# Scale columns written by ScalarE a slot before their scatter, and one-tile scatters for the last two batches

## The chip, the cores and the metric

The kernel runs on one core of one Trainium2 chip. The core has five engines: TensorE (PE, matmuls, with a weight-load part PEld), VectorE (DVE), ScalarE (ACT), GpSimd (POOL) and SyncE (SP), which issues most transfers. POOL issues the indirect transfers, those whose row numbers lie in a tile. Every engine works through its own list of instructions in order and waits on the others by semaphores. The metric is device time in microseconds (us) of one execution; less is better.

## The reference

Two stages. The first filters a sequence: `x` has 8 batches of 2496 tokens with 256 columns, and each batch is transformed along the tokens, multiplied by a filter, and transformed back. The second is a mixture of eight experts on the 19968 filtered tokens.

```python
y = np.fft.irfft(np.fft.rfft(x, axis=1) * (filt_r + 1j*filt_i), n=2496, axis=1)
x = y.reshape(8*2496, 256)
logits = x @ w_gate                        # 8 experts
e_idx = np.argmax(logits, axis=1)
gate_w = softmax(logits)[n, e_idx]
eom = 1 / (1 + np.exp(-(x @ w_output_gate)))
for e in range(8):
    mask = e_idx == e
    h = np.maximum(x[mask] @ w1[e], 0)     # 256 -> 1024
    out[mask] = gate_w[mask, None] * eom[mask, e, None] * (h @ w2[e])
```

All is float32. Each token goes through one expert only, and its row of the output is multiplied by one number, its output scale.

## The kernel before

**Tokens.** A batch is cut into 22 tiles of up to 117 tokens, 11 pairs. The filter is done as a two-step transform forwards and a two-step transform back, with a trip through memory between the steps. The last step, `inv_a` (matmul at L587, ScalarE's copy at L588), puts a pair of tiles into the ring `yring` in SBUF. The ring holds 44 rows of 258 columns a partition: two batches, so batch 7 overwrites the rows of batch 5. A row has 256 columns of the token, then the token's number (written by VectorE at L639), then its output scale.

**Routing.** When a batch is in the ring, `gates` (L624) has computed its logits, and the generator `route` takes one step a slot for five slots: the chosen expert, the place of each token in its expert's list (`dest`), and in its last step the output scale, a reciprocal that VectorE writes into the ring for all 22 tiles at once (L683).

**Scatter.** `scatter(b, q)` (L690) issues, on POOL, two indirect transfers for pair q: 117 rows each go from the ring to the sorted list `srt` in memory. Each waits for `dest` and for the ring's row.

**Experts.** The class `Experts` works through the sorted list in blocks of 512 tokens (later some of 256). A block of 512 takes 8 steps. In each step `up` multiplies by w1 (L119 to L121 into `ph`), ScalarE and VectorE read the result out of PSUM (`hh` L288, `hl` L289), and `down` multiplies by w2. Two steps after the last `up` the block's output is scaled (L331, later L327 and L328) and four indirect transfers on POOL write it to `out` (L333). The tokens of block i+2 are loaded from `srt` (`xs`, L233) in the third step of block i. All of it is unrolled. The first 12 blocks may hold only tokens of batches 0 to 3; the others wait for all scatters.

**Order.** The order on each engine is written by hand: `for n in range(-5, last + LS + TP + 1)` is a loop over slots, and `plan` names, for each slot, which function works on which batch and pair. With TP = 11, LB = 15, LI = 33, LS = 52 and last = 77:

- pair q of batch b: `inv_a` in slot 33 + 11b + q, scatter in slot 52 + 11b + q (for batch 7 one slot later); so batch 5 is scattered in slots 107 to 117, batch 6 in 118 to 128, batch 7 in 130 to 140;
- the last step of `route`, with the reciprocal, in slot 105 for batch 5, 116 for batch 6 and 128 for batch 7;
- the experts' step n in slot 105 + n: block i begins in slot 105 + 8i, and its four output transfers stand in slot 114 + 8i;
- the slot loop ends after slot 140; then the experts go on by themselves, first in `while ffn.n < 8 * NEARLY` (NEARLY = 12 blocks). The tokens of block 12, the first that waits for all scatters, are loaded in step 82, which would be slot 187.

No slot has a barrier. An engine that has no wait runs ahead of the others through its own list. From slot 105 on POOL's list holds nothing but the scatters and the output transfers.

Of the kernel before, what the change touches and what calls it, by code (L numbers as in the profile page):

```python
# [10 lines left out]
F32 = mybir.dt.float32  # L11
# [9 lines left out]
P = 128  # L21
B, S, D = 8, 2496, 256
# [3 lines left out]
NT = 22  # L26
TP = NT // 2
KP = KC // 2
# [6 lines left out]
NBLK = NFULL + 21  # L35
RING = 22
GT = 4
LATE = 7
NOID = 1 << 20

# [359 lines left out]
def build(tc, x, filt_r, filt_i, wg, wo, w1, w2, c_small, c_fb, c_ids, out):  # L400
    nc = tc.nc
    V, A, G = nc.vector, nc.scalar, nc.gpsimd
    with ExitStack() as ctx, ExitStack() as right, ExitStack() as early, ExitStack() as early_c, ExitStack() as early_x, ExitStack() as outer:
        def pool(stack, name, bufs, **kw):
            return stack.enter_context(tc.tile_pool(name=name, bufs=bufs, reuse_waits="tile", **kw))
# [3 lines left out]
        rt = pool(ctx, "rt", 1)  # L409
# [95 lines left out]
        def rows(b, t0, t1):  # L505

            o = NT * (b % 2)
            return yr[:, o + t0:o + t1]

        xt, U, Yt, T, yT, ys, lg, dest = [{} for _ in range(8)]  # L510
        XCH = [(t, min(t + 4, NT)) for t in range(0, NT, 4)]

        def load_x(b, tp):
# [82 lines left out]
        def split_y(b, tp):  # L596

            g, i = divmod(tp, GT)
            if i == 0:
                return  # L600
            if i == 1:
                ys[b, g] = [w2p.tile([P, 2 * GT, D // 32, 32], F32R, tag="ys" + c, name=f"ys{c}{b}_{tp}", bufs=1) for c in "hl"]
                split_pair(b, tp - 1)
            split_pair(b, tp)

        def split_pair(b, tp):
            g, i = divmod(tp, GT)
            h, l = [a[:, 2 * i:2 * i + 2] for a in ys[b, g]]
# [4 lines left out]
        def gates(b, tp):  # L613
            g, i = divmod(tp, GT)
            if i < GT - 1 and tp < TP - 1:
                return
# [3 lines left out]
            m = 2 * i + 2  # L620
            o = psL.tile([P, 2 * GT, 32], F32, tag="l", name=f"pl{b}_{g}")[:, 0:m, :]
            for k in range(D // 32):
# [4 lines left out]
        def route(b):  # L627
            n = 117
# [33 lines left out]
            eo = tl([NT], "eo")  # L662
# [17 lines left out]

            V.tensor_scalar(out=eo[:n], in0=eo[:n], scalar1=1.0, scalar2=None, op0=ALU.add)
            V.scalar_tensor_tensor(out=eo[:n], in0=sm[:n], scalar=1e-9, in1=eo[:n], op0=ALU.add, op1=ALU.mult)
            V.reciprocal(out=rows(b, 0, NT)[:n, :, D + 1:D + 2], in_=eo[:n].unsqueeze(2))  # L683
            dest[b] = di

        def scatter(b, q):
            di = dest[b]
            for t in (2 * q, 2 * q + 1):
                k = 39 * rows_of(t)
                i = G.indirect_dma_start(out=srt[:, :], out_offset=IndirectOffsetOnAxis(ap=di[:k, t:t + 1], axis=0),  # L690
                                         in_=rows(b, t, t + 1)[:k, 0, :], in_offset=None, bounds_check=8 * CAP - 1, oob_is_err=False)
                tc.declare_no_dep(i.ins, group="scatter", reason="tokens go to rows of their own")
                tc.add_to_no_dep_group("scatter", i.ins)
                if b >= EARLY:
                    tc.declare_no_dep(i.ins, group="early", reason="early blocks hold tokens of the first batches alone")
                    tc.add_to_no_dep_group("late", i.ins)

        LB = TP + 4
        LI = LB + TP + 7
        LS = LI + TP + 8  # L700
        last = (B - 1) * TP
        routes = []
        ffn = Experts(nc, tc, srt, w1, w2, out)

        def count(name):
# [8 lines left out]
        def table_late():  # L714

            V.tensor_copy(out=pos.unsqueeze(2), in_=st["base"][0:1, :, NT:NT + 1])
            cnt = count("cnt")
            yield from block_table(nc, tabs, cnt, numbers, "f", tables, 9, limit=NFULL - NEARLY, taken=tables[1])
            took = tabs.tile([P, 8], F32, name="took")
            V.tensor_tensor(out=took, in0=tables[1], in1=tables[3], op=ALU.add)  # L720
            V.tensor_scalar(out=took, in0=took, scalar1=2.0, scalar2=None, op0=ALU.mult)
            yield from block_table(nc, tabs, cnt, numbers, "g", tables, 8, taken=took)
            ffn.blocks += [(tables[2], i) for i in range(NFULL - NEARLY)]
            ffn.blocks += [(tables[4], i) for i in range(NBLK - NFULL)]
# [11 lines left out]
        def routing(n):  # L736
# [3 lines left out]
        plan = (  # L740
            (-5, TP, load_x), (1, TP, store_a), (LI - 4, TP, load_t), (LB - 2, KP, load_u), (LB + 3, KP, store_w),
            (LS, TP, scatter), (LB + 1, KP, filt), (LI + 1, TP, trans_y), (0, TP, fwd_a),
            (LB, KP, fwd_b), (0, 0, experts), (LB + 2, KP, inv_b), (LI + 3, TP, gates),
            (LI, TP, inv_a), (LI + 2, TP, split_y), (0, 0, routing),
        )
        for n in range(-5, last + LS + TP + 1):
            if n in (-3, 6, 13, 16):
                constants((-3, 6, 13, 16).index(n))
            if n == 3:
                nc.sync.dma_start(out=small[:, 120:664], in_=c_small[:, 120:664])  # L750
            if n == 8:
                V.tensor_copy(out=tri, in_=small[:, 256:384])
            if n in (9, 13, 16, 19):
                finish_constants((9, 13, 16, 19).index(n))
            if n == n_raw:
                early_x.close()
                ffn.open_raw(pool(right, "wraw", 1, side="right"))
            if n == n_first:
                early_c.close()
                ffn.open_first(pool(right, "xio", 1, side="right"), pool(right, "w1p", 1, side="right"))  # L760
            if n == n_ffn:
                early.close()
                tabs = pool(ctx, "tabs", 1)
                padz = tabs.tile([P, 2, ROW], F32, name="padz")
                G.memset(padz, 0.0)
                G.memset(padz[:, :, D:D + 1].bitcast(I32), NOID)
                ffn.open(pool(ctx, "wsp", 1), pool(ctx, "fio", 3), pool(ctx, "fhid", 4),
                         pool(ctx, "psh", 2, space=PSUM), pool(ctx, "pso", 1, space=PSUM))
            for off, cnt, fn in plan:
                if not cnt:  # L770
                    fn(n)
                b, i = divmod(n - off, TP)
                if fn in (gates, scatter) and n - off >= LATE * TP:
                    b, i = divmod(n - off - 1, TP)
                    if b < LATE:
                        continue
                if 0 <= b < B and i < cnt:
                    fn(b, i)
                    if fn is gates and i == TP - 1:
                        routes.append(route(b))  # L780
                        if b == EARLY - 1:
                            routes.append(table_early())
                        if b == B - 1:
                            routes.append(table_late())
            if n == n_raw + 1:
                begin = ffn.start(0, NSURE)
            if n > n_raw:
                next(begin, 0)
# [3 lines left out]
        outer.close()  # L792
        ffn.widen(pool(right, "pso2", 1, space=PSUM, side="right"))
        while ffn.n < 8 * NEARLY:
            ffn.step()

        for e in range(E + 1):
# [38 lines left out]
```

## Time and profile before

| what | value |
|---|---|
| median of 3 runs | 1422.84 us (1418.94 to 1425.73) |
| the profiled execution's own time | 1424.8 us |
| its span, first to last instruction | 1423.0 us |
| PE busy | 1316.1 us, 92% of the span |
| VectorE, ScalarE, POOL busy | 964.5, 805.4 and 439.1 us |
| TensorE's granted clock, mean | 0.960 of full speed |
| scatters (L690) | 176, 190.6 us on POOL |
| output transfers (L333) | 164, 166.0 us on POOL |

The span is the profiled execution's own time less 1.8 us ahead of the first and behind the last instruction. Busy time of matmuls is modelled at its ends, so a busy PE is not a PE at its peak. In the rows below, a bracket such as `[8.05 <-remote]` says how long the engine stood idle before the instruction and what released it; "remote" and "another core or an unknown queue" mean that the profile saw the releasing semaphore event but not who sent it, and "issue" that no waiting is recorded.

### The profile page before, as it was taken

Reading aid. Unit: us, or ns where it says so; the run is one execution under the profiler, and the core shown is the slowest. Engines: PE = TensorE matmul, PEld = TensorE weight load, DVE = VectorE, ACT = ScalarE, POOL = GpSimd, SP = SyncE. Lnnn points to the kernel's source line nnn. Section 1 sums busy time; section 2 is a strip of 40 time slices with the busy share of each in tenths; the row PEclk is TensorE's granted clock in tenths of the full one; section 3 lists DMA queues with packets and bytes.
Section 4 is the critical chain, followed back from the end, with each engine's and each line's share of the span. In section 5 each row is a group of like instructions: output and inputs, shape, how many; then the busy total and the mean of one; then the engine's idle time right before and its main releaser. Section 6 shows DMA issues by size and latency. Waiting matters only on the chain.

```text
span 1423.0 us, 22968 instructions
## 1 busy us (share of the span) xinstructions
PE 1316.1 (92%) x6596; PEld 1055.5 (74%) x6596; DVE 964.5 (68%) x1739; ACT 805.4 (57%) x1530; POOL 439.1 (31%) x425
## 2 busy tenths in 40 slices
PE   5689998998888866999999999999999999999997
PEld 2356666666566554888888888888888888999997
DVE  0346887778977453666666667666666666888885
ACT  2578887786654332455554544544555554667764
POOL 2122276677863246221221212112121121211221
PEclk8799999998999787999999999999999999999999
DMA  8999999997965134333444433334232332465521
GB/s 243 260 320 339 320 330 328 335 340 249 307 181 138 42 101 114 78 90 86 116 104 121 118 82 82 84 103 119 68 82 38 75 91 80 119 161 145 156 47 32
DMA packets 335963, 221.48 MB, mean 156 GB/s; under 512 B 209482, under 2 KB 298524, under 8 KB 335768
## 3 DMA queue, kind: packets, MB, share of 16 engines
q1 hardware_dynamic: 316408, 177.66, 45.5%
q0 software_dynamic: 19424, 42.31, 8.9%
q8 instruction: 54, 0.88, 0.3%
q14 instruction: 77, 0.63, 0.1%
HBM read 193.21 MB, written 86.42 MB: 197 GB/s over the span
## 4 chain that ended last, share of the span: by engine, by line
PE 77%; DMA 10%; DVE 5%; another core or an unknown queue 3%; issue 3%; ACT 2%; SPq 0%; POOL 0%; ACTq 0%; DVEq 0%; POOLq 0%
PE po L316 19%; PE ph L120 11%; PE ph L119 11%; PE ph L121 10%; PE po L315 8%; DMA u<-da 7%; PE py L587 3%; PE pl L624 3%; PE pb L548 3%; PE pw L566 3%; PE pa L527 2%; DMA da<-s 1%; DMA x<-in_x 1%; PE po L318 1%
## 5 line engine op out<-in xcount | busy, mean ns | idle before, releaser
L288 ACT ACTIVATE hh<-ph 128x512 fp32r<-128x512 f32 x328 | 196.5, 599 | 404.4 <-PE ph L121 340.2
L316 PE MATMUL po<-w2hl,hh 128*128 128x512 f32 x1152 | 419.1, 398 | 0.0
L289 DVE SCALAR_TENSOR_TENSOR hl<-ph,hh 128x512 fp32r<-128x512 f32 x328 | 226.1, 689 | 269.7 <-ACT hh L288 219.2
L333 POOL DMA_INDIRECT out<-ob,meta x164 | 166.0, 1012 | 743.0 <-DVE ob L328 626.7
L119 PE MATMUL ph<-xph,w1h 128*128 128x512 f32 (+1 forms) x800 | 292.2, 365 | 11.9 <-issue 6.8
L120 PE MATMUL ph<-xpl,w1h 128*128 128x512 f32 (+1 forms) x800 | 285.9, 357 | 2.9 <-issue 2.2
L121 PE MATMUL ph<-xph,w1l 128*128 128x512 f32 (+1 forms) x800 | 284.9, 356 | 1.6 <-issue 1.5
L315 PE MATMUL po<-w2hl,hl 128*128 128x256 f32 x1008 | 283.4, 281 | 0.0
L316 PEld LDWEIGHTS po<-w2hl,hh 128*128 128x128 f32 x1152 | 216.1, 189 | 47.2
L690 POOL DMA_INDIRECT srt<-yring,di x176 | 190.6, 1083 | 69.4 <-issue 48.0
L315 PEld LDWEIGHTS po<-w2hl,hl 128*128 128x128 f32 x1008 | 190.4, 189 | 9.7
L119 PEld LDWEIGHTS ph<-xph,w1h 128*128 128x128 f32 x800 | 152.5, 191 | 31.4 <-issue 10.2
L120 PEld LDWEIGHTS ph<-xpl,w1h 128*128 128x128 f32 x800 | 152.1, 190 | 31.4 <-issue 7.5
L121 PEld LDWEIGHTS ph<-xph,w1l 128*128 128x128 f32 x800 | 152.4, 190 | 24.5 <-issue 2.2
L258 DVE TENSOR_TENSOR w1l<-w1raw,w1h 128x512 fp32r<-128x512 f32 x200 | 138.8, 694 | 0.0
L258 DVE TENSOR_TENSOR w2hl<-w2raw,w2hl 128x512 fp32r<-128x512 f32 x200 | 136.9, 684 | 0.4
L257 ACT CAST w1h<-w1raw 128x512 fp32r<-128x512 f32 x200 | 124.2, 621 | 0.1
L257 ACT CAST w2hl<-w2raw 128x512 fp32r<-128x512 f32 x200 | 123.0, 615 | 0.0
L554 POOL TENSOR_TENSOR vs<-vs,fi 128x512 f32<-128x512 f32 x56 | 72.2, 1290 | 161.3 <-ACT vs L551 153.4
L548 PEld LDWEIGHTS pb<-u,fb 128*128 128x128 f32 x320 | 59.3, 192 | 81.5 <-issue 34.3
L527 PE MATMUL pa<-x,small 117*120 117x512 f32 (+1 forms) x176 | 98.0, 648 | 17.7 <-ACT s L529 11.5
L548 PE MATMUL pb<-u,fb 128*128 128x256 f32 x320 | 86.3, 392 | 28.2 <-DMA u<-da 24.6
(180 smaller groups left out, 1798.5 us busy)
## 6 DMA issues: line engine op xcount, KB each, us to landing
w1raw<-in_moe_w SPq DMA_DIRECT2D x200, 256.0 KB
w2raw<-in_moe_w SPq DMA_DIRECT2D x200, 256.0 KB
u<-da SPq DMA_DIRECT2D x80, 256.0 KB
dw<-w SPq DMA_DIRECT2D x80, 256.0 KB
da<-s SPq DMA_DIRECT2D x80, 240.0 KB
t<-dw SPq DMA_DIRECT2D x80, 240.0 KB
x<-in_x SPq DMA_DIRECT2D x40, 468.0 KB
xs<-srt SPq DMA_DIRECT2D x128, 128.0 KB
```

Source lines behind the costliest of these rows:

```text
L119: nc.tensor.matmul(out, lhsT=a[0], rhs=b[0], start=first, stop=False)
L120: nc.tensor.matmul(out, lhsT=a[0], rhs=b[1], start=False, stop=False)
L121: nc.tensor.matmul(out, lhsT=a[1], rhs=b[0], start=False, stop=last)
L257: self.nc.scalar.copy(out=h, in_=r)
L258: self.nc.vector.tensor_tensor(out=lo, in0=r, in1=h.bitcast(F32), op=ALU.subtract)
L288: nc.scalar.activation(out=h, in_=ph, func=AF.Relu)
L289: nc.vector.scalar_tensor_tensor(out=l, in0=ph, scalar=0.0, in1=h.bitcast(F32), op0=ALU.max, op1=ALU.subtract)
L315: nc.tensor.matmul(o[:, 0, :], lhsT=hl, rhs=self.w2hl[g][:, f, 0], start=False, stop=False)
L316: nc.tensor.matmul(o, lhsT=hh, rhs=self.w2hl[g][:, f], start=first, stop=last)
L333: d = nc.gpsimd.indirect_dma_start(out=self.out[:, :], out_offset=IndirectOffsetOnAxis(ap=s["meta"][:, 2 * u + v, 0:1].bitcast(I32), axis= ...
L548: nc.tensor.matmul(ps[:, i, :], lhsT=fb[2 * kp + i], rhs=u[:, i, :], start=True, stop=True)
L690: i = G.indirect_dma_start(out=srt[:, :], out_offset=IndirectOffsetOnAxis(ap=di[:k, t:t + 1], axis=0), in_=rows(b, t, t + 1)[:k, 0, :], in ...
```

## The change

For batches 5, 6 and 7 the reciprocal is written into a small tile of its own (`rc`), not into the ring. ScalarE copies it from there into the ring's scale column: for batch 5 two tiles at a time, in the slot ahead of that pair's scatter; for batches 6 and 7 one tile at a time. These two batches no longer scatter a pair in a slot: their 44 tiles are in a list `singles`, one taken in each slot from slot 118 on, each followed by the copy for the next. After the slot loop the rest of the list is taken in the experts' steps. Batches 0 to 4 are as before.

```diff
+PACED = 5
+SINGLE = 6
...
-            V.reciprocal(out=rows(b, 0, NT)[:n, :, D + 1:D + 2], in_=eo[:n].unsqueeze(2))
+            if b < PACED:
+                V.reciprocal(out=rows(b, 0, NT)[:n, :, D + 1:D + 2], in_=eo[:n].unsqueeze(2))
+            else:
+                scale[b] = rt.tile([P, NT], F32, tag="rc", name=f"rc{b}", bufs=2)
+                V.reciprocal(out=scale[b][:n], in_=eo[:n])
             dest[b] = di
 
+        def put_scale(b, t0, t1):
+
+            A.copy(out=rows(b, t0, t1)[:117, :, D + 1:D + 2], in_=scale[b][:117, t0:t1].unsqueeze(2))
+
+        def scale_pair(b, q):
+            if PACED <= b < SINGLE:
+                put_scale(b, 2 * q, 2 * q + 2)
+
         def scatter(b, q):
+            if b < SINGLE:
+                scatter_tiles(b, 2 * q, 2 * q + 2)
+
+        def scatter_single():
+
+            if singles:
+                b, t = singles.pop(0)
+                scatter_tiles(b, t, t + 1)
+            if singles:
+                b, t = singles[0]
+                put_scale(b, t, t + 1)
+
+        def scatter_tiles(b, t0, t1):
             di = dest[b]
-            for t in (2 * q, 2 * q + 1):
+            for t in range(t0, t1):
...
+        singles = [(b, t) for b in range(SINGLE, B) for t in range(NT)]
...
-            (LB, KP, fwd_b), (0, 0, experts), (LB + 2, KP, inv_b), (LI + 3, TP, gates),
+            (LB, KP, fwd_b), (0, 0, experts), (LS - 1, TP, scale_pair), (LB + 2, KP, inv_b), (LI + 3, TP, gates),
...
+            if n == LS + SINGLE * TP - 1:
+                put_scale(SINGLE, 0, 1)
+            if n >= LS + SINGLE * TP:
+                scatter_single()
...
         while ffn.n < 8 * NEARLY:
+            scatter_single()
             ffn.step()
```

## Rows read from the trace of the kernel before

**Rows 1.** The page: TensorE and the other engines, busy over the whole span.

```profile
PE 1316.1 (92%) x6596; PEld 1055.5 (74%) x6596; DVE 964.5 (68%) x1739; ACT 805.4 (57%) x1530; POOL 439.1 (31%) x425
```

**Rows 2.** Windows between output transfers: length, PE, PEld, DVE, ACT, POOL busy, PEclk, DMA share, GB/s.

```profile
383.00:407.50 24.50, 15.93 (x65) 10.87 (x65) 22.89 (x48) 13.25 (x28) 16.70 (x16) 0.86 0.73 197
407.50:449.40 41.90, 38.11 (x200) 29.73 (x200) 28.82 (x54) 21.60 (x43) 17.38 (x16) 0.96 0.55 151
449.40:498.50 49.10, 40.90 (x191) 30.91 (x190) 27.44 (x51) 20.19 (x41) 19.99 (x20) 0.79 0.32 78
498.50:537.10 38.60, 26.89 (x163) 23.82 (x162) 20.79 (x49) 13.13 (x29) 17.87 (x18) 0.82 0.36 99
537.10:581.00 43.90, 30.58 (x145) 24.98 (x144) 18.84 (x62) 11.51 (x24) 19.88 (x20) 0.73 0.32 85
581.00:607.60 26.60, 24.76 (x145) 21.95 (x144) 14.27 (x28) 11.39 (x23) 7.85 (x8) 0.94 0.45 116
607.60:630.60 23.00, 23.00 (x116) 19.30 (x115) 14.19 (x24) 12.13 (x25) 4.08 (x4) 1.00 0.31 70
630.60:653.00 22.40, 22.40 (x114) 18.81 (x113) 15.10 (x27) 11.38 (x23) 3.93 (x4) 1.00 0.48 124
```

**Rows 3.** Window of the long stage behind, same columns.

```profile
607.60:900.00 292.40, 292.40 (x1461) 245.55 (x1460) 196.24 (x337) 149.19 (x289) 51.55 (x53) 1.00 0.40 100
```

**Rows 4.** Windows around POOL's unbroken runs: length, POOL busy (transfers), PEclk, DMA share, GB/s.

```profile
403.80:429.80 26.00, 17.38 (x16) 0.98 0.62 165
449.40:475.30 25.90, 19.99 (x20) 0.76 0.53 133
498.50:519.00 20.50, 15.77 (x16) 0.80 0.42 115
537.10:562.90 25.80, 19.88 (x20) 0.72 0.53 141
581.00:591.10 10.10, 7.85 (x8) 1.00 0.72 164
607.60:614.40 6.80, 4.08 (x4) 1.00 0.84 173
```

**Rows 5.** Timeline: start, us, instruction; a result and who took it up late.

```profile
505.61 0.27 PE L624 MATMUL pl<-ysl,wq 128*128 128x192 f32 x1
...
517.81 0.38 DVE L625 STREAM_TRANSPOSE lg<-pl 128x192 f32<-128x192 f32 x1 [12.57 <-remote]
...
543.69 0.40 PE L121 MATMUL ph<-xph,w1l 128*128 128x512 f32 x1
...
548.14 0.60 ACT L288 ACTIVATE hh<-ph 128x512 fp32r<-128x512 f32 x1 [8.05 <-remote]
...
565.70 0.60 ACT L288 ACTIVATE hh<-ph 128x512 fp32r<-128x512 f32 x1 [16.96 <-remote]
```

**Rows 6.** Timeline of PE: the last transform in two slots, and gate matmuls.

```profile
412.13 1.02 PE L587 MATMUL py<-t,small 120*128 120x512 f32 x2
...
415.80 1.02 PE L587 MATMUL py<-t,small 120*128 120x512 f32 x2
...
420.86 0.28 PE L624 MATMUL pl<-ysh,wq 128*128 128x256 f32 x1
...
422.55 1.02 PE L587 MATMUL py<-t,small 80*128 80x512 f32 x2
```

**Rows 7.** Timeline of ScalarE: its smallest copy.

```profile
525.37 0.19 ACT L665 COPY si<-so 128x8 f32<-128x8 f32 x1
```

**Rows 8.** Groups by shape, 537.1 to 581 and 630.6 to 653.06: busy us, mean ns.

```profile
L289 DVE SCALAR_TENSOR_TENSOR hl<-ph,hh 128x512 fp32r<-128x512 f32 x8 | 5.5, 688 | 24.1 <-ACT hh L288 15.6 <-issue 8.4
L289 DVE SCALAR_TENSOR_TENSOR hl<-ph,hh 128x512 fp32r<-128x512 f32 x8 | 5.5, 692 | 7.3 <-ACT hh L288 6.0 <-issue 1.3
```

**Rows 9.** Waits, 449.4 to 498.5: us in total, times, longest.

```profile
ACT yring L588 <- DMA srt<-yring,di: 10.7, 1, 10.7
```

**Rows 10.** DMA queues, 564 to 567: packets, MB, share of 16 engines.

```profile
q0 software_dynamic: 5, 0.00, 0.2%
```

More of the change, by code (lines that the diff above doesn't have):

```diff
@@ L508, in rows @@
             return yr[:, o + t0:o + t1]
-        xt, U, Yt, T, yT, ys, lg, dest = [{} for _ in range(8)]
+        xt, U, Yt, T, yT, ys, lg, dest, scale = [{} for _ in range(9)]
         XCH = [(t, min(t + 4, NT)) for t in range(0, NT, 4)]
```

## The prediction

> **What bounds the kernel now.** I read the page first: TensorE is busy 92% of the span, no other engine above 68% [rows 1]. That is an average over stages, so the second view is the table of windows, cut where a block's output transfers begin on POOL. Seven cuts, from 407.5 to 630.6, are the outputs of one block after another, so each window holds eight experts' steps. The reader is to see two things. From 607.6 on TensorE has no idle time, 292.4 of 292.4 us, and a block takes 22.4 us, 2.8 a step [rows 2, 3]: time gained ahead of 607.6 reaches the end unshortened. And just ahead of it, the same eight steps take 49.1, 38.6, 43.9 and 26.6 us, with every engine less busy than before and a mean granted clock down to 0.73, so that TensorE, whose levels are 1.2 and 2.4 GHz, spent part of the time at the lower one after standing idle [rows 2].
>
> How much of that is work? A slot that also does `inv_a` takes 415.80 - 412.13 = 3.67 us, 0.87 more than a bare step; fourteen gate matmuls run from 420.86 to 422.55, 0.12 each, so a group of 16 costs 1.9 [rows 6]. Block 0's window holds slots 115 to 122: six `inv_a` and two groups of gates, 22.4 + 5.2 + 3.8 = 31.4; so 17.7 of its 49.1 us are lost. Block 1 holds one smaller group: 24.2, so 14.4 lost. The next three hold none: 21.5, 4.2 and 0.6 lost. The sum is 58.4 us.
>
> Third view, why: POOL's runs. After 407.5 POOL's list holds only scatters and outputs. The scatters of a batch wait for its reciprocal alone, so POOL runs ahead until it meets four output transfers whose block is not ready, stands there, and then issues these four and all scatters listed up to the next block's outputs without a gap. The windows around the unbroken runs show 20, 16, 20 and 8 transfers, in 25.9, 20.5, 25.8 and 10.1 us, four of them outputs each time, then a run of four outputs alone, 5.2 us of a 6.8 us window [rows 4]. Set against the losses:
>
> - run 25.9 us, lost 17.7
> - run 20.5, lost 14.4
> - run 25.8, lost 21.5
> - run 10.1, lost 4.2
> - run 5.2, lost 0.6
>
> So what is lost is about the run less 6 us. Fourth view, the timeline inside runs: the gates' result was ready by 505.9 and VectorE took it up at 517.81, where the run ended; ScalarE took up an `up` result ready by 544.1 only at 548.14, and its next at 565.70, after 16.96 us of idleness, 3 us behind the run's end [rows 5]. The releaser is not named. I read it so: in a long unbroken run of POOL's indirect transfers, the other engines are released late. Full transfer queues are not the reason: in those windows the share is 0.42 to 0.53, against 0.84 in the short run that costs nothing [rows 4].
>
> **The change part by part.** *The waits.* A scatter now needs a copy that ScalarE makes a slot earlier, in its own order. So POOL can't run ahead of ScalarE by more than a slot. Behind the waiting scatter on POOL stand later scatters and the output transfers, nothing else; the outputs need their own slot's ScalarE work anyway. The reciprocal precedes its first copy by a slot, so ScalarE should not stand for it.
>
> *The runs that remain.* Singles come one in 2.8 us and take 1.3 us of POOL (26.0 us for 20 transfers, 25.9 [rows 4]). Four outputs take 5.2; in that time two singles come due, then a third at about 7 to 8: a run of about 9 us, where the rule above gives 3. Outputs meet singles in slots 122, 130, 138, 146 and 154. In slot 114 they meet pairs, one pair each 3.67 us: 4 + 2 + 2 + 2 transfers, some 13 us, rule 7. Together 22. But a held-up ScalarE now releases no further scatters, so a run can't feed itself. I estimate half, 11 us; the bounds are 0 and six times the 4.2 that the 4 + 4 run cost, 25.
>
> *The first run.* Batch 5's first 16 scatters run from 407.8 to 429.7 without a gap. The window 407.5 to 449.4 is 41.9 us; its eight slots with `inv_a` and two groups of gates are 29.4 + 3.8 = 33.2, so 8.7 are lost there [rows 2, 6]. Spreading gives back between 0 and 8.7; I take 3, since a window of 26 us with 16 transfers kept the clock at 0.98 [rows 4], so this run hurt least.
>
> *The copies.* 11 for batch 5 and 44 for the others: 55, none in the trace. The nearest is ScalarE's 0.19 us copy of 8 elements a partition [rows 7]; 55 x 0.19 = 10.5 us of ScalarE. It is busy 11.4 of 22.4 us in a clean block [rows 2], which hides them; without that cover they cost 10.5. I take 1.
>
> *The reciprocal* writes 22 elements a partition as before; nothing. *The later end of the scatters:* the last is now in step 56, not 35. The first load that needs all of them is in step 82, 26 x 2.8 = 73 us behind; nothing.
>
> *The sum* against the profiled execution's own 1424.8: less 58.4, plus 11, less 3, plus 1, is 1375.4. The median of the runs is 2.0 lower; as that is taken without this profile, the losses are no product of profiling. I say **1374 us**. With the bounds: all given back, 1424.8 - 58.4 - 8.7 - 2 = 1356; least, 58.4 - 25 - 10.5 = 22.9 gained, 1400.
>
> **The rivals.**
>
> *Outputs with scatters behind them are the harm, not the length.* The four costly runs all begin with outputs; the 16 scatters alone cost 8.7 at most. Then each of six meetings keeps more than the 4.2 of its cheapest case. At 5 to 6 each, 30 to 36 remain and 22 to 28 are gained: 1395 to 1401. Against: four outputs with their block's loads cost 0.6 [rows 2].
>
> *A price per transfer.* From 449.4 on 50 scatters are issued; 58.4 / 50 = 1.17 us each, whenever they come. Then the change only spreads the loss: 1423, or 1433 with the copies uncovered, mostly no change. For it: the three long runs cost 17.7 / 20, 14.4 / 16 and 21.5 / 20, about 0.9 to 1.1 us a transfer alike. Against: in 383 to 407.5 POOL was busy 16.7 of 24.5 us, and VectorE still 22.9 [rows 2]; and output transfers cost nothing.
> VectorE's subtraction takes 688 ns in a window with a long run and 692 in a clean one, so it is the start that is late, not the execution [rows 8]. The Trainium skill speaks against the change here: its page "SBUF — State Buffer", section "Who interferes with whom", has only the port pair of VectorE and GpSimd in contention, and says of the others "PE and ACT never wait on anyone". By that rule POOL's runs can't hold ScalarE, the late releases have another cause, and the change gains nothing, 1423. The trace does not agree: ScalarE's long idle times stand in the runs [rows 5].
>
> *Slower: the ring.* Batch 7's `inv_a` overwrites batch 5's rows, whose scatter now leaves ScalarE's hands four slots ahead of it rather than running early. One such wait, 10.7 us, is already there [rows 9]. If a scatter took longer than four slots, 14.7 us, to be done, each of 11 pairs would stretch its slot. To lose 0.5% beyond the gain of 49, w us a slot must be 56 / 11 = 5.1, which wants 4 x (3.67 + 5.1) = 35 us a scatter; at w = 6 the time is 1374 + 66 = 1440. Against: 1.1 us behind the longest run's end the scatter queue holds five packets in 3 us [rows 10].
>
> **How the numbers follow.** Runs are the cause and go: 0.66, 1356 to 1392. Meetings with outputs keep their harm: 0.14, 1392 to 1405. Price per transfer, or another cause altogether: 0.13, 1416 to 1433, of which 0.11 within the bound. The ring: 0.07, about 1440. About 0.5%, 7 us, can be told from no change. Faster 0.80, same 0.11, slower 0.09. The range 1356 to 1405 holds the first two cases; their 0.80 is what I want of it.
>
> **What would show it.** In the changed profile: no unbroken run on POOL above ten transfers after 407; idle gaps of a slot between singles; blocks' windows of at most 34, 27, 25, 25 and 25 us where there were 49.1, 38.6, 43.9, 26.6 and 23.0; a clock near 1.0 there; no idle time of 8 us or more on ScalarE with an unnamed releaser; scatters ending some 60 us after slot 140; the ScalarE copies at 0.2 us. I am wrong if short runs still come with late releases, if new gaps stand at `inv_a`'s copies with the scatter queue as releaser, or if ScalarE's own lateness holds up scatters, and with them block 12's loads.

## The result, and the profile after

The changed kernel takes 1381.21 us (median of 6 runs, 1377.60 to 1385.82) against 1421.43 us for the kernel before (6 runs, 1411.40 to 1425.73): a ratio of 0.9735, 95% interval 0.9709 to 0.9762. The profiled execution took 1385.8 us, its span is 1383.9. The direction of the gain is as forecast, the size is 40 us rather than 49.

In the rows of the changed kernel the scatter is L717, the output transfer L335, ScalarE's new copy L694, `up` L121 to L123, `hh` L290, `hl` L291. First the page, which answers to [rows 1]:

```profile
PE 1297.8 (94%) x6596; PEld 1050.3 (76%) x6596; DVE 962.1 (70%) x1739; ACT 808.9 (58%) x1585; POOL 442.7 (32%) x425
```

and the new copies, taken together by their line (count, shortest, median and longest ns, first and last start, shapes):

```profile
L694 ACT COPY yring<-rc x55: 174/190/232, 416.8 to 613.0; 117x1 f32<-117x1 f32 x44, 117x2 f32<-117x2 f32 x11
```

ScalarE has 55 instructions more (1585 against 1530), of 190 ns each. The windows between the outputs of one block and the next answer to [rows 2] (length, PE, PEld, DVE, ACT, POOL busy, PEclk, DMA share, GB/s):

```profile
407.50:449.10 41.60, 41.19 (x224) 33.95 (x225) 33.86 (x67) 23.99 (x53) 20.49 (x18) 0.94 0.60 161
449.10:482.30 33.20, 32.55 (x191) 27.09 (x190) 26.82 (x51) 20.78 (x49) 14.31 (x14) 1.00 0.45 106
482.30:512.80 30.50, 27.58 (x163) 24.77 (x162) 20.74 (x49) 13.42 (x36) 12.61 (x12) 0.89 0.40 111
512.80:540.50 27.70, 24.69 (x146) 22.08 (x145) 18.74 (x64) 12.15 (x32) 12.60 (x13) 0.94 0.37 93
540.50:568.20 27.70, 24.64 (x146) 21.93 (x145) 14.15 (x28) 12.19 (x33) 13.62 (x14) 0.94 0.50 134
568.20:595.70 27.50, 24.67 (x116) 20.50 (x115) 14.09 (x24) 12.78 (x34) 12.70 (x12) 0.94 0.38 94
595.70:619.70 24.00, 22.65 (x114) 18.72 (x113) 14.93 (x27) 11.78 (x29) 12.18 (x11) 1.00 0.56 147
619.70:642.00 22.30, 22.30 (x114) 18.80 (x113) 15.16 (x28) 11.45 (x23) 4.52 (x5) 1.00 0.31 66
```

Where 49.1, 38.6, 43.9, 26.6, 23.0 and 22.4 us stood, the six blocks now take 33.2, 30.5, 27.7, 27.7, 27.5 and 24.0. Against the prediction's work of 31.4, 24.2 and four times 22.4, what is lost is 1.8, 6.3, 5.3, 5.3, 5.1 and 1.6: 25.4 us, where 58.4 were lost. So 33 came back. The last two blocks lose more than before: the singles have moved into them. The two windows that lose least are not those with the shortest runs. Block 0's outputs stand in the longest run of all: a pair of batch 5 ahead of them and two pairs behind make ten transfers from 445.85 to 459.44 us, 13.6 us, and that window loses 1.8. These are the first output and the last scatter of that run:

```profile
449.11 1.01 POOL L335 DMA_INDIRECT out<-ob,meta  x1 [0.35 <-ACT ob L333]
...
458.45 0.99 POOL L717 DMA_INDIRECT srt<-yring,di  x1 [0.30 <-issue]
```

The clock row is read with the length: the granted mean is 0.89 to 0.94 in the four middle windows, so TensorE is at the lower of its two levels for a part of each. One of these meetings in the timeline shows why (this answers to [rows 5]):

```profile
540.47 0.99 POOL L335 DMA_INDIRECT out<-ob,meta  x1 [4.56 <-ACT ob L333]
...
543.35 0.19 ACT L694 COPY yring<-rc 117x1 f32<-117x1 f32 x1
544.21 0.39 PE L123 MATMUL ph<-xph,w1l 128*128 128x512 f32 x1
544.35 0.98 POOL L335 DMA_INDIRECT out<-ob,meta  x1 [0.30 <-issue]
...
548.15 0.99 POOL L717 DMA_INDIRECT srt<-yring,di  x1 [0.30 <-issue]
550.84 0.60 ACT L290 ACTIVATE hh<-ph 128x512 fp32r<-128x512 f32 x1 [7.31 <-remote]
551.81 0.99 POOL L717 DMA_INDIRECT srt<-yring,di  x1 [2.66 <-ACT yring L694]
552.22 0.50 PE L121 MATMUL ph<-xph,w1h 128*128 128x512 f32 x1 [1.82 <-DVE hl L291]
```

Four outputs and three singles run unbroken from 540.47 to 549.1. The `up` result was complete by 544.6; ScalarE took it up at 550.84, after 7.31 us without work and with a releaser that is not named. TensorE then waits for what ScalarE and VectorE owe it. The old picture is still there, only shorter.

The trace's semaphore events say what that wait was for, although the view prints only "remote": ScalarE waits there for a semaphore that TensorE alone raises. Three `up` and `down` matmuls that raise it ended, by their records, at 544.60, 545.90 and 547.41 us; the three raises are recorded at 550.82, 550.94 and 551.02. In the meeting before, the ends are 516.97, 518.27 and 519.78 and the raises 523.14, 523.26 and 523.34. So it is TensorE's signal that comes late, several at once. The ends of matmuls are modelled, and elsewhere the trace lacks some of these events, so this is shown for these two meetings and not for every one.

The waits from 407.5 to 620 (us in total, times, longest) show both sides:

```profile
ACT hh L290 <- remote: 26.2, 5, 7.3
...
POOL srt L717 <- ACT yring L694: 65.5, 26, 8.0
```

The second row is the change at work: POOL waits for the copies 26 times and no longer runs ahead. The first is what is left of the harm; it was 37.4 us, 7 times, 17.0 at most in the kernel before, from 407.5 to 607.6. No wait of ScalarE's `yring` for a transfer is left, where 10.7 us stood [rows 9].

### The profile page after: what moved, and what is told of

The parts are those of the page before. It is cut to its first block, busy times and chain, and to the rows that moved or that the text cites. A ratio compares the mean times of both kernels' runs of the same rounds, so it can differ in the third digit from the quotient of the medians.

```text
span 1383.9 us, 23072 instructions
## 1 busy us (share of the span) xinstructions
PE 1297.8 (94%) x6596; PEld 1050.3 (76%) x6596; DVE 962.1 (70%) x1739; ACT 808.9 (58%) x1585; POOL 442.7 (32%) x425
## 4 chain that ended last, share of the span: by engine, by line
PE 79%; DMA 11%; issue 3%; DVE 3%; ACT 2%; another core or an unknown queue 1%; SPq 1%; POOL 0%; ACTq 0%; DVEq 0%; POOLq 0%
PE po L318 19%; PE ph L123 11%; PE ph L121 11%; PE ph L122 11%; PE po L317 8%; DMA u<-da 8%; PE pb L550 3%; PE py L589 3%; PE pw L568 3%; PE pa L529 3%; PE pl L626 3%; PE po L320 1%; DMA da<-s 1%; DMA x<-in_x 1%
## 5 line engine op out<-in xcount | busy, mean ns | idle before, releaser
L290 ACT ACTIVATE hh<-ph 128x512 fp32r<-128x512 f32 x328 | 196.0, 598 | 379.9 <-PE ph L123 338.8
L318 PE MATMUL po<-w2hl,hh 128*128 128x512 f32 x1152 | 414.6, 394 | 0.0
L291 DVE SCALAR_TENSOR_TENSOR hl<-ph,hh 128x512 fp32r<-128x512 f32 x328 | 225.6, 688 | 251.2 <-ACT hh L290 209.8
L335 POOL DMA_INDIRECT out<-ob,meta x164 | 166.5, 1015 | 651.9 <-DVE ob L330 597.0
L121 PE MATMUL ph<-xph,w1h 128*128 128x512 f32 (+1 forms) x800 | 291.9, 365 | 10.1 <-DVE hl L291 7.0
L123 PE MATMUL ph<-xph,w1l 128*128 128x512 f32 (+1 forms) x800 | 285.0, 356 | 0.0
L717 POOL DMA_INDIRECT srt<-yring,di x176 | 193.9, 1102 | 110.0 <-ACT yring L694 65.5
L121 PEld LDWEIGHTS ph<-xph,w1h 128*128 128x128 f32 x800 | 152.1, 190 | 28.7 <-DVE hl L291 8.9
L122 PEld LDWEIGHTS ph<-xpl,w1h 128*128 128x128 f32 x800 | 151.8, 190 | 27.5 <-issue 3.4
L123 PEld LDWEIGHTS ph<-xph,w1l 128*128 128x128 f32 x800 | 152.2, 190 | 23.5
L550 PE MATMUL pb<-u,fb 128*128 128x256 f32 x320 | 86.6, 393 | 32.7 <-DMA u<-da 25.4
```

Source lines behind the costliest of these rows:

```text
L121: nc.tensor.matmul(out, lhsT=a[0], rhs=b[0], start=first, stop=False)
L122: nc.tensor.matmul(out, lhsT=a[0], rhs=b[1], start=False, stop=False)
L123: nc.tensor.matmul(out, lhsT=a[1], rhs=b[0], start=False, stop=last)
L290: nc.scalar.activation(out=h, in_=ph, func=AF.Relu)
L291: nc.vector.scalar_tensor_tensor(out=l, in0=ph, scalar=0.0, in1=h.bitcast(F32), op0=ALU.max, op1=ALU.subtract)
L318: nc.tensor.matmul(o, lhsT=hh, rhs=self.w2hl[g][:, f], start=first, stop=last)
```

## Experiments

One table first. "Lost" is, over the six blocks from block 0's outputs on, the time above the 145.2 us of work (31.4 + 24.2 + 4 x 22.4), from the profiled execution. Ratios are to runs of the kernel before on the same chip.

| kernel | median us | ratio, 95% interval | lost us |
|---|---|---|---|
| before | 1421.4 | | 58.4 |
| changed | 1381.2 | 0.9735, 0.9709 to 0.9762 | 25.4 |
| singles, no hold | 1430.7 | 1.0073, 1.0034 to 1.0111 | 60.4 |
| hold, all pairs | 1388.9 | 0.9781, 0.9708 to 0.9855 | 30.2 |
| copies alone | 1424.9 | 1.0020, 0.9978 to 1.0062 | 52.9 |
| singles kept off the outputs | 1366.2 | 0.9622, 0.9549 to 0.9694 | 7.7 |
| the same, block 0's outputs later | 1366.7 | 0.9611, 0.9547 to 0.9676 | |
| before + memset behind scatters | 1367.3 | 0.9583, 0.9536 to 0.9630 | 4.9 |
| before + tiny memset | 1424.2 | 1.0010, 0.9974 to 1.0045 | 51.1 |
| before + memset behind scatters and outputs | 1361.7 | 0.9549, 0.9510 to 0.9587 | 3.4 |
| changed + memset behind scatters | 1379.1 | 0.9674, 0.9625 to 0.9723 | 16.8 |
| changed + memset behind scatters and outputs | 1360.0 | 0.9598, 0.9544 to 0.9652 | 2.0 |

The theory: a long unbroken run of POOL's indirect transfers makes the other engines' releases late. The rivals are those of the prediction: the meeting with outputs, a price per transfer, the hold as such.

### The change taken apart

**One-tile scatters without the hold.** The reciprocal goes into the ring as before and the copies are left out.

```diff
-            A.copy(out=rows(b, t0, t1)[:117, :, D + 1:D + 2], in_=scale[b][:117, t0:t1].unsqueeze(2))
+            pass
```

> One part alone: batches 6 and 7 go one tile a slot, but the scales are written into the ring by VectorE as before, so no copy holds a scatter back. Run theory (a long unbroken run of POOL's indirect transfers makes the other engines start late, by about the run less 6 us): POOL runs ahead again, meets four outputs and then has 8 singles behind them, 12 transfers or 15.6 us a block, 9.6 lost in each of four blocks and some 16 in the first: about 1417, little better than before. If one tile a slot is what counts, not the hold: about 1381, as the changed kernel. Price per transfer: 1421.

It is 0.7% slower than before, 1430.7. Without the hold POOL runs ahead all the same; a block's four outputs are followed at once by some eight singles, 10 to 13 transfers in a row, and the windows are 37.8, 37.2, 33.8, 33.2, 33.2 and 30.4. In the four middle blocks such a run costs 10.8 to 13.0 us, more than the 9.6 expected. Spreading the same scatters over more blocks is worth nothing by itself. By its time alone this kernel would also fit a price per transfer; the doses below decide that.

**The hold without singles.** `SINGLE = 8`: batches 6 and 7 are scattered in pairs, each pair behind its copy.

> The other part alone: ScalarE's copies hold back the scatters of batches 5, 6 and 7, which all stay pairs. A pair takes POOL 2.6 us of a step's 2.8, so behind four outputs the run hardly ends before the next outputs. Run theory: four meetings with runs of 10 us and more, limited only by ScalarE's own lateness, 8 to 15 us lost in each: 1390 to 1410. Meeting theory (only scatters next to outputs harm): four meetings of 5 us and nothing else, about 1375 to 1381. Price per transfer: 1421.

1388.9: some four fifths of the gain. Of the change's two parts it is the hold that carries most of it.

**The copies without the hold.** The kernel before, with 55 copies of the same size into a tile that nobody reads:

```diff
+            A.copy(out=idle[b][:117, t0:t1], in_=scale[b][:117, t0:t1])
```

> The kernel before (scales written into the ring by VectorE, pairs, nothing held) with the 55 small copies added on ScalarE at the changed kernel's places, into a tile that nobody reads. Prediction's step: 0 to 10.5 us more, I took 1: 1419 to 1430. A gain would say that the copies, not the hold, are the cause.

1424.9, no difference from the kernel before. The copies cost nothing that can be measured, and give nothing.

### Where the rest stands

**Singles kept off the outputs.** No single in the three steps behind a block's outputs; 1, 1, 2, 1, 1 in the other five.

```diff
-            if singles:
-                b, t = singles.pop(0)
+            ph = (ffn.n - 1) % 8
+            due = {4: 1, 5: 1, 6: 2, 7: 1, 0: 1}
+            for b, t in singles[:due.get(ph, 0)]:
                 scatter_tiles(b, t, t + 1)
...
```

> The changed kernel, with no single in the three slots behind a block's outputs: one each in the next five, two in the middle one of them. Same transfers, same copies; the scatters end in step 72, still ahead of block 12's loads in step 82. Run theory and meeting theory: the 5 us that each of four blocks still loses go, 18 to 23 us less than the changed kernel, about 1359. Price per transfer: no change, 1381. If the loss comes from the scatters' writes in memory beside the token loads behind the outputs: also about 1359.

The windows of its first four blocks, columns as above:

```profile
447.90:485.20 37.30, 34.71 (x192) 28.27 (x191) 27.42 (x51) 20.77 (x50) 16.26 (x16) 0.95 0.40 97
485.20:510.20 25.00, 24.58 (x163) 22.38 (x162) 20.66 (x49) 13.32 (x34) 10.60 (x10) 1.00 0.45 126
510.20:533.10 22.90, 22.87 (x145) 20.45 (x144) 18.11 (x62) 11.98 (x30) 10.64 (x10) 1.00 0.42 100
533.10:555.60 22.50, 22.50 (x145) 20.40 (x144) 14.87 (x30) 12.21 (x31) 10.64 (x10) 1.00 0.55 148
```

Where singles no longer touch outputs, the loss is gone and the clock is at its upper level (1.00). Only block 0's window, whose outputs still meet pairs of batch 5 (twelve transfers in a row, 16.1 us), loses 5.9. So most of the 25 us stand where singles meet outputs.

**Block 0's outputs four slots later**, in the same kernel, to take that meeting apart as well.

```diff
+            if i == 0:
+                self.plan.setdefault(self.n + 4, []).append((self.send, (s, ob, u)))
```

> The third experiment's kernel (singles kept off the three slots behind outputs), and block 0's four outputs issued four slots later, behind batch 5's last pairs; the singles begin after them and end in step 78. Run theory: the run of outputs and pairs behind slot 114, 13 us, falls apart, and the first block's window comes down from 37.3 to about 32: 5 us less than the third experiment, 1361. Price per transfer: no change from it, 1366.

1366.7, no difference, where 5 us less were expected. Block 2's outputs start at 508.13 us where they started at 510.24, too little to be told in the medians.

### How much of what does it take

**Doses in the clean stage.** The changed kernel, with transfers of ring rows into an array of their own, which nobody reads, added to single blocks of the stage where TensorE is otherwise never idle: 4, 8 or 16 right behind a block's four outputs; 8 or 16 alone, four steps behind the outputs; 16 whose row numbers all lie out of range, so that no row is moved; 24 memsets of POOL; 16 of 32 rows.

```diff
+            what, m = DOSE[b]
...
+            if k == (4 if "alone" in what else 0):
...
+                    copies(m, far if "far" in what else spare, 32 if "few" in what else 117, D if "short" in what else ROW)
```

> The changed kernel with added transfers in the clean stage, into a spare list in memory that nobody reads; every second block has one kind, the block between has none. Behind the outputs: 4, 8 and 16 copies of 117 rows. Alone, held by a ScalarE copy to the middle of the block: 8 and 16 copies. Behind and alone, 16 copies with all row numbers out of range, so that POOL issues them but no row is moved. Behind, 24 memsets of POOL, no transfer. Alone, 16 copies of 32 rows. Lost against a clean block of 22.2 us by the run theory (run less 6): 4.4, 9.6, 20, 4.4, 14.8 for the first five; with nothing moved the same 20 and 14.8 if issuing is the cause, 0 if moving the rows is; memsets 0; few rows 14.8 if the number of transfers counts, under 5 if the rows do. Meeting theory: the two alone cost 0. Price per transfer (1.17 us): 4.7, 9.4, 18.7, 9.4, 18.7.

The windows, in the order 4, 8, 16 behind outputs; 8 alone and 16 alone (two blocks each, since they reach into the next); 16 behind outputs and 16 alone with rows out of range; 24 memsets. A block without addition takes 22.42, two take 44.84.

```profile
789.16:813.00 23.84, 22.65 (x114) 18.82 (x113) 14.86 (x27) 11.31 (x23) 7.92 (x8) 1.00 0.37 88
835.42:863.47 28.05, 24.26 (x114) 19.76 (x113) 14.96 (x27) 11.30 (x23) 12.23 (x12) 0.94 0.50 136
885.88:927.72 41.84, 27.29 (x114) 22.07 (x113) 15.05 (x27) 11.41 (x23) 20.06 (x21) 0.80 0.41 114
950.14:994.98 44.84, 44.84 (x226) 37.66 (x225) 30.25 (x53) 22.90 (x46) 16.59 (x16) 1.00 0.47 117
994.98:1052.44 57.46, 48.72 (x226) 39.80 (x225) 30.43 (x53) 23.17 (x46) 25.60 (x25) 0.91 0.42 108
1052.44:1094.66 42.22, 28.00 (x114) 22.56 (x113) 15.08 (x27) 11.40 (x23) 19.83 (x21) 0.80 0.14 25
1117.07:1173.21 56.14, 47.50 (x226) 38.87 (x225) 30.51 (x53) 23.24 (x46) 25.54 (x24) 0.94 0.30 70
1173.21:1195.63 22.42, 22.42 (x114) 18.83 (x113) 15.12 (x27) 11.41 (x23) 16.63 (x28) 1.00 0.31 64
```

Behind outputs 4, 8 and 16 cost 1.4, 5.6 and 19.4; eight alone cost 0.0, sixteen alone 12.6. By the transfers in a row, outputs counted, that is 0.0 to 1.4 for eight, 5.6 for twelve, 12.6 for sixteen and 19.4 for twenty. The price grows much faster than the number, so there is no price per transfer; and a run without outputs at its head does harm too, so the meeting alone is not the cause. Memsets that keep POOL busier (16.63 us of a block) than the run of twelve does (12.23) cost nothing. Each of these figures is from one block, or two, of one execution; the next kernel has one case twice, and its two figures are 2.9 us apart. The two rows with rows out of range are the sharpest: 19.8 and 11.3 us, about as much as with rows moved (19.4 and 12.6), though over 23 us in the first of them the queues did next to nothing (packets, MB, share of 16 engines):

```profile
q0 software_dynamic: 832, 0.01, 2.2%
```

It is the issuing on POOL that harms, not the moving. Sixteen transfers of 32 rows cost 12.7, the same again.

**Pauses in the run.** The same, with ten transfers behind the outputs and POOL memsets of 128x512 (0.55 us) between them; and ten of the plain kind, issued by POOL or by SP.

```diff
+            what, m, every, gap = DOSE[b]
...
+                if every and j % every == every - 1:
+                    for _ in range(gap):
+                        G.memset(padz[:, :, 0:D], 0.0)
```

> The changed kernel with ten added transfers of 117 rows behind the four outputs of every second block of the clean stage, into a spare list that nobody reads, 14 in a row with the outputs. Block 14 and again block 28: no pause, 18.2 us; between the 5.7 that 12 in a row cost and the 19.4 of 20, 8 to 10 us lost. Block 16: a POOL memset of some 0.6 us behind each. Block 18: two. Block 20: three behind every second. Block 22: six behind every fifth. Block 24: ten plain transfers from POOL (112 rows, no row numbers). Block 26: the same ten from SP. If what harms is that no pause comes, the blocks with pauses lose nothing; if it is how much of the time POOL issues, small pauses help little (1.3 of 1.9 us: 6 to 9 lost) and only the larger ones do. If row numbers matter, plain ones lose nothing; if any transfer that POOL issues does it, 8 to 10; SP's nothing under every theory but one that blames the transfers themselves.

The windows: no pause; one memset behind each, and two behind each (two blocks each time); six memsets behind every fifth; ten plain transfers from POOL; no pause, repeated. A clean block takes 22.34 here.

```profile
792.94:828.70 35.76, 24.59 (x114) 20.20 (x113) 15.08 (x27) 11.30 (x23) 13.88 (x15) 0.86 0.31 78
851.03:896.25 45.22, 44.92 (x226) 37.59 (x225) 30.02 (x53) 22.72 (x45) 24.35 (x29) 1.00 0.50 121
896.25:940.91 44.66, 44.66 (x226) 37.59 (x225) 30.19 (x53) 22.71 (x45) 29.15 (x38) 1.00 0.50 122
985.81:1012.40 26.59, 24.14 (x114) 20.02 (x113) 15.01 (x27) 11.42 (x23) 20.68 (x26) 0.94 0.57 153
1034.73:1057.07 22.34, 22.34 (x113) 18.81 (x113) 15.16 (x27) 11.41 (x23) 9.25 (x15) 1.00 0.41 100
1124.06:1156.93 32.87, 24.86 (x114) 20.23 (x113) 15.09 (x27) 11.41 (x23) 14.39 (x15) 0.90 0.34 82
```

Lost: 13.4, 0.5, 0.0, 4.3, 0, and 10.5 in the repeat; 8 to 10 had been expected without a pause. POOL has more to do with the memsets in between (24.35 us in those two blocks), yet the loss falls from over 10 us to half a one. Three memsets behind every second cost 0.2. Nine unbroken transfers (four outputs and five) still cost 4.3. Plain transfers cost nothing, from SP or from POOL, which spends 0.53 us on each of the ten, one behind the other without a gap. So what follows on the distance between transfers is said of indirect ones.

### The run broken without any hold

If that is so, the change's copies, its small tile and its list of singles are not needed. Three kernels put a memset of POOL behind each scatter of batches 5 to 7 in the kernel before, and touch nothing else.

```diff
                 if b >= EARLY:
...
                     tc.add_to_no_dep_group("late", i.ins)
+                if b >= 5:
+                    G.memset(ffn.padz[:, :, 0:D], 0.0)
```

> The kernel before, with one memset of a 128x512 tile on POOL (0.55 us) behind each scatter of batches 5, 6 and 7; pairs, no copies, nothing that ties POOL to ScalarE. If only the unbroken run counts, nearly all of the 58.4 us comes back: 1421 - 58 = 1363, up to 1370 if the four outputs at the head of a run still cost 1 to 1.5 each time. If tying POOL to ScalarE's order is what helped, or each transfer has a price, nothing comes back: 1417 to 1425, and longer if the memsets' 36 us of POOL are in the way.

> The same with a memset of 128x2, the shortest work that POOL can be given (some 0.1 us). If any work of POOL between two transfers ends the run, it is equal to the long memset, about 1363. If the length of the pause counts, 0.1 of 0.55 us gives back a fifth or less: 1410 to 1420.

> The long memset behind each scatter of batches 5 to 7 and also behind each output transfer of the first blocks. If the four outputs at the head of a run are a short run of their own with a small price, this is 1 to 7 us below the kernel with memsets behind scatters alone. If they cost nothing, equal.

The long memset gives 1367.3. In its windows TensorE has hardly a gap, though POOL is busy nearly all the time (29.87 of 34.00 us in the first):

```profile
444.70:478.70 34.00, 34.00 (x201) 28.47 (x200) 27.33 (x51) 21.71 (x45) 29.87 (x36) 1.00 0.51 120
478.70:509.80 31.10, 30.26 (x200) 27.50 (x199) 27.02 (x66) 14.59 (x31) 27.31 (x33) 1.00 0.60 159
509.80:543.80 34.00, 33.92 (x214) 30.35 (x214) 27.83 (x69) 16.78 (x32) 29.86 (x37) 1.00 0.45 121
543.80:572.30 28.50, 28.14 (x148) 23.58 (x147) 16.66 (x28) 15.26 (x30) 14.55 (x17) 1.00 0.43 111
```

(The first three windows are long because the outputs wait behind the scatters in POOL's list; 200 and more matmuls stand in each. Read PE's busy time, which fills it.) Block 6's outputs start at 594.72 us where they started at 653.06. Of these 58.3 us, 53.5 come back in the six blocks, where 58.4 were lost; block 0's outputs start 4.8 earlier: there the first run's loss is back too, in an execution that was 2.7 us behind (see *The first run* below). So neither the hold nor ScalarE's order is needed.

The tiny memset gives nothing: 1424.2 (its profiled execution, 1410.3, is the shortest of its ten runs, and loses 51 us in the six blocks all the same). Three lines of POOL's timeline in each kernel say why. With the tiny one:

```profile
536.19 0.99 POOL L690 DMA_INDIRECT srt<-yring,di  x1 [0.19 <-issue]
537.18 0.12 POOL L698 MEMSET padz<- 128x2 f32 x1
537.49 0.99 POOL L690 DMA_INDIRECT srt<-yring,di  x1 [0.19 <-issue]
```

and, in the kernel with the long one:

```profile
526.10 0.99 POOL L690 DMA_INDIRECT srt<-yring,di  x1 [0.18 <-issue]
527.09 0.54 POOL L698 MEMSET padz<- 128x512 f32 x1
527.81 0.99 POOL L690 DMA_INDIRECT srt<-yring,di  x1 [0.18 <-issue]
```

The tiny memset goes into the 0.30 us that stood between two transfers anyway: from start to start it is 1.30 us, as without it. With the long one it is 1.71. So work of POOL that leaves the distance of the transfers as it is gives nothing. That a longer distance helps without any memset is what the singles kept off the outputs showed. Memsets behind the first blocks' outputs as well give 1361.7. Their interval overlaps that of the kernel without them, so the difference is not shown by these two.

### The same in the changed kernel

Memsets behind the scatters, as above, added to the changed kernel ("e3" below is the kernel with singles kept off the outputs).

> The changed kernel with the long memset behind each scatter of batches 5 to 7. Its 25.4 us of loss at the meetings should go by the run theory, as each run there becomes single transfers with pauses behind the four outputs: 1381 - 25 = 1356, up to 1366 where e3 stands. If the meetings with outputs cost by themselves, or the hold makes the loss, it stays at 1378 to 1384.

1379.1, not the 1356 to 1366 of the run theory. Memsets behind the scatters take only 8.6 of the 25.4 us here. ScalarE still stands:

```profile
543.07 0.19 ACT L694 COPY yring<-rc 117x1 f32<-117x1 f32 x1
548.98 0.60 ACT L290 ACTIVATE hh<-ph 128x512 fp32r<-128x512 f32 x1 [5.71 <-remote]
```

At that place POOL issued four outputs and one single, 540.20 to 546.34, without a pause, and singles with pauses behind. Either those five are too many, or the hold makes the loss. The last kernel tells these two apart; it adds this:

```diff
                 self.tc.add_to_no_dep_group("out", d.ins)
+                if self.n < 90:
+                    nc.gpsimd.memset(self.padz[:, :, 0:D], 0.0)
```

> The changed kernel with the long memset behind each scatter of batches 5 to 7 and also behind each output transfer of the first blocks. With the memset behind scatters alone 1379.1 was measured, and ScalarE still stood late by 5 to 7 us at each meeting, from four outputs and one single without a pause onwards. If those five transfers are what still costs, the rest of the loss goes now: 1356 to 1362. If tying the scatters to ScalarE at the outputs makes the loss, it stays: 1374 to 1381.

1360.0, with the hold and the meetings as they were. Its windows:

```profile
446.00:477.40 31.40, 31.40 (x189) 26.46 (x188) 26.21 (x48) 19.88 (x45) 22.79 (x28) 1.00 0.43 102
477.40:502.50 25.10, 24.68 (x164) 22.39 (x163) 21.09 (x49) 13.62 (x37) 19.50 (x25) 1.00 0.49 137
502.50:525.60 23.10, 23.02 (x146) 20.48 (x145) 19.52 (x61) 12.24 (x32) 19.06 (x25) 1.00 0.43 109
525.60:549.10 23.50, 23.50 (x150) 21.22 (x149) 15.30 (x31) 13.16 (x35) 21.17 (x27) 1.00 0.60 161
549.10:571.40 22.30, 22.30 (x114) 18.80 (x113) 14.63 (x26) 12.07 (x30) 20.16 (x24) 1.00 0.46 110
```

31.4, 25.1, 23.1, 23.5 and 22.3 us: the work that the prediction had worked out (31.4 for block 0 to the tenth), with 2 us lost in six blocks. This one and the kernel before with memsets behind both are the shortest of all; they ran on different chips, and their ratios (0.960 and 0.955) can't be told apart.

## Why the prediction came out as it did

**The loss and its place: right.** 58.4 us were said to be lost ahead of block 6's outputs; spacing the transfers in the kernel before gave 53.5 of them back in the six blocks, with nothing else changed. Two readings on the way were loose and moved no sum: the cut at 407.5 is the start of batch 5's scatters, not of a block's outputs, and POOL was not less busy in the slow windows (41 to 46% of the first three, 41% of the one ahead).

**The waits: right.** POOL waits for the copies (65.5 us, 26 times); the runs are six transfers where batch 5 begins, the ten that were reckoned at block 0's outputs, seven at the next four and eight at block 5's; between meetings scatters come by ones and twos with gaps of 1 to 4 us; the last ends at 614.8 us. No new wait at the ring, so that rival falls.

**The runs that remain: the term that was mis-sized.** I put 11 us, with 25 as the bound; 25.4 were measured. The step that failed is the halving, from 22 to 11, because "a run can't feed itself": no row was behind it, and the runs came as they had been counted, seven transfers at the four middle meetings, at 5.1 to 6.3 us each. The 22 themselves are near 25.4 only because two errors of the rule "lost is about the run less 6 us" nearly cancel: 1.8 us came for the run of ten in slot 114 where it gave 7, and 23.6 for the other five meetings where it gave 15. So length alone doesn't set the loss in this stage: runs of ten and eight (13.6 and 10.6 us) cost 1.8 and 1.6, runs of seven (8.7 us) three times as much. The doses don't explain that; there a run of eight cost 1.4 at most, below the rule. The rule's lowest point was no run either: of the four outputs from 607.62 on, the second waited 2.02 us for ScalarE. With the halving went the expected windows of 34, 27, 25, 25 and 25 us (33.2, 30.5, 27.7, 27.7 and 27.5 came; only the first kept to them) and the clock near 1.0.

**The first run: 3 us were taken, 7.4 measured.** Slot 106 begins the stretch that batch 5's scatters fill, and its `inv_a` in the kernel before and in the changed one is

```profile
408.45 1.02 PE L587 MATMUL py<-t,small 120*128 120x512 f32 x2
...
415.55 1.02 PE L589 MATMUL py<-t,small 120*128 120x512 f32 x2
```

From there to block 0's outputs it is 40.97 us before (to 449.42) and 33.56 after (to 449.11). The same stretch takes 33.4 to 34.5 us in the nine kernels that hold or space batch 5's scatters and leave block 0's outputs in their place (the two with doses are among them), and 37.8 to 43.1 in the four whose POOL runs ahead. So nearly all of the 8.7 us that the prediction had as its bound came back. The window from 407.5 hides it (41.9 and 41.6 us), since the changed kernel's execution came to slot 106 7.1 us later, ahead of its first copy at 416.8. That the clock was 0.98 over this run was no sign that it hurt little.

**The copies: 1 us taken, none measured**, in a kernel of their own. ScalarE's idle time covers them, as was said.

**The sum.** The terms as measured, 58.4 - 25.4 + 7.4, give 40.4 us where 49.4 were forecast: too much by 14.4 for the runs that remain, too little by 4.4 for the first run and by 1 for the copies. The profiled spans differ by 39.1, and that has two more parts, neither in the prediction: the 7.1 us by which the changed kernel came later to slot 106, and 5.8 us from the stage behind, where a block took 22.24 instead of 22.42 us. They nearly cancel, and that is luck: with either alone the difference of the spans would be 33 or 46 us.

**The rivals.** *Meetings with outputs* was right about the number, 5 to 6 us, at four of the six meetings, and wrong about the cause: sixteen transfers with no outputs at their head cost 12.6 in the clean stage and 7.4 as the first run, and with the memsets all six meetings together cost 2.0, though outputs and scatters meet as before. *A price per transfer* falls: eight alone are free, and the same transfers with pauses are nearly free. That rows moved in SBUF are not the cause is shown by the transfers that moved none. The sentence of the Trainium skill weighed there ("SBUF — State Buffer", section "Who interferes with whom": "PE and ACT never wait on anyone") was taken too widely in the prediction. It speaks of access to SBUF, and of that the runs show nothing against it: durations stay as they are [rows 8], and rows moved in SBUF are not needed. What ScalarE waits for, 19.35 us in one place of the kernel with tiny memsets, is a signal, and the loss came and went with the spacing of POOL's transfers.

**Open.** How issuing on POOL delays TensorE's signal: no experiment reached it. Loading of code was not varied either; packets of 16 KB of the instruction queue q8 come in the clean stage too, nine in ten blocks of the changed kernel, and no time is lost there. Also open is what makes the meetings of blocks 1 to 4 dear. In the changed kernel with memsets behind scatters five unbroken transfers with paused ones behind cost 3.1 to 5.3 us in each of these blocks and nothing in blocks 0 and 5; the same pattern cost 0.5 in the clean stage, and 4.9 us in all in the kernel before with memsets. So the lengths that are harmless in one stage can't be taken over to another.

## What to carry to other kernels

Where engines stand idle with an unnamed releaser while POOL issues indirect transfers back to back, space the transfers: 1.7 us from start to start instead of 1.3 took the loss away here, and a filler on POOL is enough, if it is longer than the gap that is there already. Space every indirect transfer in the list: in the changed kernel the scatters alone gave 8.6 of 25.4 us, scatters and outputs together nearly all. Before making one engine wait for another to pace it, try the filler; and if the pacing stays, keep it off the other bursts in the same list. A rule fitted to a few runs should not be scaled by a factor that no row shows. And compare two executions from the same piece of work, not from the same time.

## What was not expected of the hardware

An indirect transfer whose rows are all out of range harms as much as one that moves 117 rows (19.8 and 19.4 us for sixteen behind outputs), at 2.2% of the queues' time. What comes late is then the signal of another engine, TensorE, whose work was done.

The block's pitch in the clean stage, TensorE without a gap at clock 1.00, differs by 0.8% between the profiled executions of these kernels: 22.24 us in the changed kernel and in five of its variants, 22.42 in the kernel before and in five others, among them two variants of the changed kernel, 22.34 and 22.29 in the remaining two. What sets it was not found; over the stage it is worth 5.8 us, more than some edits. The six executions at 22.24 come to slot 106 at 411.5 to 417.4 us, the six at 22.42 at 404.1 to 411.1, so what is gained behind was lost ahead; whether the two hang together is not shown.
